# Attention on one core: VectorE's score units placed in ScalarE's sets of PSUM banks, and half of x turned by TensorE

## The chip, the cores and the metric

The kernel runs on one core of a Trainium2 chip. Five engines work side by side, each with its own queue of instructions in a fixed order: TensorE (PE in the profile; its weight loads are PEld), VectorE (DVE), ScalarE (ACT), GpSimd (POOL) and SyncE (SP), which here issues most of the transfers between memory and the core's SBUF. Matmuls write to PSUM, eight banks of 512 fp32 columns on 128 partitions. Semaphores order the engines against each other. The metric is the time of one execution on the device in microseconds (us); lower is better.

## The reference

Two attention blocks over the same x (2048 rows of 512 columns, bf16), each with its own weights, 32 heads of 16 columns, are mixed by a gate of each row.

```python
# block A: full softmax attention, no mask
scores = jnp.einsum("bhqd,bhkd->bhqk", q, k) * (Dh ** -0.5)
p = _softmax(scores, axis=-1)
o = jnp.einsum("bhqk,bhkd->bhqd", p, v)            # then @ A_wo
# block B: each row looks at itself and at 7 rows before it, two apart
W, dil = 8, 2
logits = jnp.einsum("bhsd,bhswd->bhsw", q, kg) * scale   # masked before row 0
attn = _softmax(logits, axis=-1)
o = jnp.einsum("bhsw,bhswd->bhsd", attn, vg)       # then @ B_wo
# the mix
g = _sigmoid((x * gate_w).sum(-1, keepdims=True))
return g * a + (1 - g) * b
```

Block A's exponentials are the bulk: 32 heads x 2048 x 2048.

## The kernel before

**Units, sets and terms.** Block A is worked in 32 periods (line 1263), each with 512 rows of q and four heads. A unit is the score tile of one head for 128 keys and 512 rows of q: one matmul with 32 rows of the array (a strip) into one PSUM bank. A period has 64 units, so there are 2048. A unit is exponentiated in one of two ways. ScalarE reads a set of neighbouring banks, called ring, in one ACTIVATE with exp and writes pT (`emit_fill` line 1419, `act_source` line 1443). There are two sets in turn, rA of three banks and rB of two. VectorE takes units in groups of four, the four heads of one tile of 128 keys (`make_quad`, line 1559; a quad in the code): a conversion of the scores to integers that are the bits of a bf16 near the exponential (dt<-m_ps, one for each unit), then two integer additions over all four units (dt<-dt, the terms; OFFS and WTS at the top of the kernel), so that three terms with weights approximate the exponential. TensorE multiplies pT by v, or the three terms by v and two weighted copies of v (vd_row), and accumulates in the bank acc. Only the last TD = 4 tiles of keys of a period can go to VectorE, since only for these is there a weighted v.

**Banks.** rA three, rB two, acc one, and two single banks m0 and m1 (shown as m_ps). The single banks serve VectorE's score units, and also all projections of q, k and v, block B's projections and sums, and the output projections.

**Block B.** For each of 16 tiles of 128 rows (`b_tile`, line 896): projections on TensorE, k and v stored to memory and loaded again shifted (ksh, vsh), products and sums on GpSimd, softmax, and the weighted sum over the eight rows as matmuls with an identity (`vsum`, line 1075). From tile RELIEF = 6 on, part of the sums is done by VectorE (lred).

**The head.** x is loaded transposed into xT by eight transposing DMAs (`x_load`, line 596). The first weights come on ScalarE's queue into w0 and are rearranged by ScalarE. Ten warm matmuls run meanwhile. `k_proj` with first=True (line 686) projects the first heads' k for four quarters of the rows, VectorE takes the largest absolute value of each (kmax_all), ScalarE copies k to kt_all, VectorE applies a bias from the maximum (kadd), and `q_proj` (line 809) gives q, which VectorE spreads over the strips (shuffles and a bit mask). Then the first set can be filled.

**The order.** The Python program plans the whole order: `Sched` (line 167) keeps for each engine a clock, the pending operations with durations and due times, and slots for every buffer; at each step it commits the operation that can start first, or among near ones that with the earliest due time. `Policy` draws a few settings from a seed, one for each stretch of 8 us of the plan (CHOICES, line 69). `pe_source` (line 1352) offers fills and products, `d_source` and `start_quad` (lines 1618, 1527) open a new group of four for VectorE when the estimated work of both engines allows. `zero_pass` (line 1629) adds matmuls with zeros where TensorE would be too idle. The order is fixed when the program is built; at run time each engine runs its queue and waits on semaphores.

Most instructions go through one wrapper, so the profile shows L509 for nearly all of them, and groups are told apart by tiles: ring, m_ps, acc (PSUM), pT, dt, kt_all, qt, xT (SBUF).

Of the kernel before, what the change touches and what calls it, by code (L numbers as in the profile page):

```python
# [20 lines left out]
DH = 16  # L21
NG = 8
W = 8
# [8 lines left out]
TD = 4  # L32
# [48 lines left out]
RELIEF = 6  # L81
# [47 lines left out]
class Policy:  # L129
    __slots__ = ("full", "press", "quads", "backlog", "heed", "near", "shift", "conv", "ring", "rng", "wobble", "warm", "tight", "late", "whole", "split")  # L130

    def __init__(self, seed):
        self.full, self.press, self.quads, self.backlog, self.heed = 5, -2000.0, 3, 3000.0, True
        self.near, self.shift, self.conv, self.ring, self.wobble, self.warm = 60.0, 0.0, -5000.0, 480.0, 0.0, 0.0
        self.tight, self.late, self.whole, self.split = 600.0, 2000.0, False, False
        self.rng = random.Random(seed)
        if seed:
# [16 lines left out]
            self.warm = pick(0.0, 0.04, 0.08, -0.03)  # L154

# [290 lines left out]
def kernel(  # L446
# [143 lines left out]
    S_.t["DVE"] = 2500.0  # L590
    S_.t["ACT"] = 2500.0
# [4 lines left out]
    def x_load(half):  # L596

        def s():
            lo, hi = half * S // 2, (half + 1) * S // 2
            for c in range(DC):  # L600
                SP.dma_start(out=xT[:, c, lo:hi], in_=x2d[lo:hi, c * 128:(c + 1) * 128], transpose=True)
        return s
# [30 lines left out]
    for kind, lo in (("k", D), ("q", 0)):  # L633
        w0[kind] = const.tile([128, DC, G1], BF16, name=f"w{kind}0")
# [11 lines left out]
    load("x0", x_load(0), 8100.0)  # L646
    load("x1", x_load(1), 13600.0)
    ld["x1a"] = S_.add(Op("SP", lambda: None, dur=1.0, due=-8.0, lat=13000.0, name="ld_x1a"))
    load("bw", dma(bw[:], B_wqkv.rearrange("(c p) n -> p c n", p=128)), 20500.0)
# [4 lines left out]
    load("gw", gw_load, 22000.0)  # L654
    load("wv", dma(wv[:, :, G1:D], a_w3[:, :, 2 * D + G1:3 * D]), 24000.0)
# [22 lines left out]
    S_.t["PE"] = 7800.0  # L678
    xt_ops = {sc: [ld[f"x{sc // 2}"]] for sc in range(NC)}
# [6 lines left out]
    def k_proj(m, sc, due, first=False):  # L686
        lent = first and sc >= 2
        if lent and not early:
            early["hold"] = Hold("rB")
        hold = early["hold"] if lent else Hold("m")  # L690
        st = {}

        def part(c0, c1):
            def s():
                if c0 == 0 and lent:
                    if sc == 2:
                        early["ps"] = ps.tile([128, 2, QW], FP32, tag="rB", bufs=1, name="ring")
                    st["pk"] = early["ps"][:, sc - 2, :]
                elif c0 == 0:
                    st["pk"] = misc_ps(hold, [128, QW])[:]  # L700
# [17 lines left out]
        slow = 2 if first and sc == 0 else 1  # L718
        p1 = Op("PE", part(0, 2), mms=COL4 * (2 * slow), deps=([ld["x1a"]] if lent else xt_ops[sc]) + [ld[("k", m)]], due=due, acq=[] if lent and sc > 2 else [hold], not_before=0.0 if first else due - 5000.0,
                begun=[early["op"]] if lent and sc > 2 else [], name="k1")  # L720
        p2 = Op("PE", part(2, DC), mms=COL4 * (2 * slow), deps=[p1] + (xt_ops[sc] if lent else []), due=due, name="k2")
        for o in (p1, p2):
            S_.add(o)
        if first:
            r = S_.add(Op("DVE", red, dur=700.0, deps=[p2], due=due, name="kred"))
            e = S_.add(Op("ACT", evac, dur=650.0, deps=[p2, r] + k_evs.get(m, [])[-1:], due=due, rel=[] if lent and sc == 2 else [hold], name="kev"))
            if lent and sc == 2:
                early["op"] = p1
            if lent and sc > 2:
                early["next"] = p2  # L730
# [78 lines left out]
    def q_proj(c_, f, due):  # L809
# [15 lines left out]
        def evac():  # L825
            st["qt"] = sb(hq, [128, 2, QW], BF16, "qt")
            V.tensor_copy(out=st["qt"][:, 1, :], in_=st["q"][:])
# [3 lines left out]
        def spread():  # L831
            v = st["qt"][:].bitcast(I32)
            V.stream_shuffle(out=v[:, 0, :], in_=v[:, 1, :], mask=LOWER)
            V.stream_shuffle(out=v[:, 1, :], in_=v[:, 1, :], mask=UPPER)

        def fold():
            for b in range(2):
                v = st["qt"][:, b, :].bitcast(U16)
                V.tensor_scalar(out=v, in0=v, scalar1=rowmask[:, b:b + 1], scalar2=None, op0=ALU.bitwise_and)
        ops = [Op("PE", part(0, 2), mms=COL4 * 2, deps=xt_ops[c_] + [ld[("q", f)]], due=due, acq=[hold, hq], name="q1"),  # L840
               Op("PE", part(2, DC), mms=COL4 * 2, due=due, name="q2"),
               Op("DVE", evac, dur=683.0, allow=300.0, rel=[hold], name="qev"),
               Op("DVE", spread, dur=860.0, allow=2000.0, name="qsh"),
               Op("DVE", fold, dur=486.0, lock=True, allow=2000.0, name="qabs")]
        S_.chain(ops)
        qb_ops[(c_, f)] = ops[1]
        for b in range(2):
            qt_ops[(c_, 2 * f + b)] = (ops[-1], hq)
# [47 lines left out]
    def b_tile(t, due):  # L896
# [190 lines left out]
        f = [Op("PE", vsum(c), mms=[("f", None, 132)] * W, allow=4000.0 if c == 0 else -3000.0, acq=[hb, obt_hold[t]] if c == 0 else [],  # L1087
# [127 lines left out]
    def lent_final(tt, due):  # L1215
# [6 lines left out]
        def step(lo, hi):  # L1222
            def s():
                if not lo:
                    lent["ps", tt] = ps.tile([128, 3 - tt, QW], FP32, tag=tag, bufs=1, name="ring")[:, 0, :]
# [126 lines left out]
    def pe_source(e):  # L1352
# [5 lines left out]
        n = 3 if ring_i[0] == 0 else 2  # L1358
        w = S_.slots[res].when()
        us = act_units(n)  # L1360
        if us and w < INF:
# [3 lines left out]
            if r < INF and S_.slots["pTA" if n == 3 else "pTB"].when() < INF:  # L1365
# [3 lines left out]
                op = Op("PE", None, mms=[("r", u[2], 512) for u in us], name="fillA")  # L1369
                op.fn = lambda us=us, res=res, n=n, op=op: emit_fill(us, res, n, op)  # L1370
# [3 lines left out]
        if pv_wait:  # L1374
# [8 lines left out]
            if whole or full:  # L1383
                a = acc_ready(p)
                if a is not None:
                    vs = [vp_ops[(u[1], 4 * periods[p][1] + u[2])].vis for u in batch]
                    if all(v is not None for v in vs):
# [8 lines left out]
                        used = [sum(w >= INF for w in S_.slots[tag].free) for tag in ("pTA", "pTB")]  # L1396
                        outl.append((op, r, batch[0][3] + (2000.0 if sum(used) < S_.policy.full else S_.policy.press)))
# [21 lines left out]
    def emit_fill(us, res, n, op):  # L1419
# [6 lines left out]
        op.acq = [ring, us, res, n]  # L1426

    def after_fill(op):
        ring, us, res, n = op.acq
# [11 lines left out]
        filled.append(dict(ring=ring, us=us, res=res, n=n, vis=op.vis))  # L1441

    def act_source(e):
# [3 lines left out]
        tag = "pTA" if f_["n"] == 3 else "pTB"  # L1447
# [6 lines left out]
        def fn():  # L1454
            f_["hold"] = Hold(tag)
            f_["hold"].k = S_.slots[tag].take()
            pT = sb(f_["hold"], [128, f_["n"], QW], BF16, "pT")
# [3 lines left out]
        def after(o):  # L1461
            filled.pop(0)
            S_.slots[f_["res"]].give(0, o.vis)
# [55 lines left out]
    quad_at = [0]  # L1519
    quad_end = [None]  # L1520
# [38 lines left out]
    def make_quad(p, t, late):  # L1559
# [6 lines left out]
        aops, fops = [], []  # L1566
        heads = [0, 1, 2, 3]

        def strip():
            after = {u[2] for u in act_units(3 if ring_i[0] == 0 else 2)}  # L1570
            return min(heads, key=lambda j: (max(S_.pe_busy[j], S_.t["PE"]), j in after, j))
        for n_ in range(4):
            hold = Hold("m")
            st = {}

# [4 lines left out]
            def fill(n_=n_, hold=hold, st=st):  # L1580
# [3 lines left out]
                st["s"] = misc_ps(hold, [128, QW])  # L1584
                for _ in range(f_.zeros):
                    mm_pass(st["s"], True, True)
                mm(st["s"][:], kt_all[32 * j:32 * j + 32, i, t * 128:(t + 1) * 128],
                   qt_tiles[periods[p]][32 * j:32 * j + 32, :], True, True, tile_position=(32 * j, 0))

            def conv(n_=n_, st=st):  # L1590
                if n_ == 0:
                    term_tile()
                V.tensor_scalar(out=q["terms"][0][:, st["j"], :], in0=st["s"][:], scalar1=EXP_MULT, scalar2=EXP_ADD,
# [17 lines left out]
        def done(o):  # L1611
            d_busy[0] -= 1
            q["vis"] = o.vis
            pvd_ready.append(q)
# [3 lines left out]
    def d_source(e):  # L1618
        if e == "PE" and d_busy[0] < S_.policy.quads:
# [3 lines left out]
            if dve + max(0.0, S_.t["DVE"] - S_.now) < S_.policy.backlog and S_.now > 22000.0:  # L1623
# [5 lines left out]
    def zero_pass(now):  # L1629
# [5 lines left out]
        if p is None and not front[0]:  # L1635
            mm_pass(ps.tile([128, 3, QW], FP32, tag="rA", bufs=1, name="ring")[:, 0, :], True, True)
# [66 lines left out]
    reds0 = [k_proj(0, sc, 30.0 + sc, first=True) for sc in range(NC)]  # L1703
    k_rows(0, reds0, 40.0, 1, 35000.0)
# [38 lines left out]
```

## Time and profile before

| | |
|---|---|
| time, median of 3 runs | 744.76 us (744.65 to 745.12) |
| the profiled execution | 744.69 us, its span 742.9 us |
| busy: PE, DVE, ACT, POOL | 695.6, 652.9, 719.2, 436.0 us |
| exponentials on ScalarE (pT<-ring) | 626 instructions, 711.7 us |
| conversions on VectorE (dt<-m_ps) | 484 instructions, 319.8 us |
| terms on VectorE (dt<-dt) | 242 instructions, 166.2 us |
| first exponential, end of the last one | 19.46 us, 732.20 us |
| mean granted TensorE clock | 1.000 |

The span runs from the first to the last instruction; the time holds about 1.8 us more. Rows give tiles as out<-in, then the shape, the count, the busy time together, the mean of one in ns, and the idle time of the engine just before them with what ended it. The mean of one holds its latency, during which the next has begun already; where the pace matters, starts are compared with starts.

### The profile page before, as it was taken

What the parts mean: (1) busy time and instruction counts of PE and PEld (TensorE: products, weight loads), DVE (VectorE), ACT (ScalarE), POOL (GpSimd) and SP (SyncE); (2) the same over time, 40 slices, a digit from 0 to 9 for tenths busy, and PEclk for the clock granted to TensorE, in tenths of its full rate; (3) what the DMA queues carried; (4) which work ended last, traced back from release to release, by engine and by line L of the source; (5) the groups of instructions that cost most, each with busy time, mean ns of one, the idle gap of its engine ahead of it and who ended that gap; (6) DMA issues with size and microseconds to landing.
All of it is one profiled execution on the core that took longest, in us unless ns stands there. A gap on an engine that the chain in (4) does not pass through costs nothing.

```text
span 742.9 us, 19546 instructions
## 1 busy us (share of the span) xinstructions
PE 695.6 (94%) x8110; PEld 247.9 (33%) x8110; DVE 652.9 (88%) x1177; ACT 719.2 (97%) x658; POOL 436.0 (59%) x456
## 2 busy tenths in 40 slices
PE   8899999999999989999999999999999999999897
PEld 2332332323323323333323333333333333323233
DVE  3888999798898898989999999989998988897963
ACT  2999999999999999999999999999999999999994
POOL 1066455756556666666655656657656557666660
PEclk9999999999999999999999999999999999999999
DMA  9413020120331201212132311121131113222100
GB/s 217 132 20 119 2 72 2 61 70 15 96 49 59 72 2 60 69 58 73 57 77 25 115 35 39 58 73 58 57 101 58 63 53 102 73 72 71 59 30 29
DMA packets 76232, 47.42 MB, mean 64 GB/s; under 512 B 37232, under 2 KB 73584, under 8 KB 76144
## 3 DMA queue, kind: packets, MB, share of 16 engines
q1 hardware_dynamic: 74288, 45.52, 20.9%
q8 instruction: 63, 1.03, 0.6%
q10 hardware_dynamic: 1856, 0.66, 0.3%
q14 instruction: 25, 0.20, 0.1%
HBM read 37.75 MB, written 6.32 MB: 59 GB/s over the span
## 4 chain that ended last, share of the span: by engine, by line
ACT 64%; PE 17%; issue 15%; DVE 5%; DVEq 0%; ACTq 0%
ACT pT L509 63%; PE m_ps L509 6%; PE acc L509 5%; PE ring L509 5%; DVE dt L509 2%; PE warm L509 1%; ACT lg L509 1%; DVE kt_all L509 0%; DVE accT L509 0%; DVE qt L509 0%; DVE kmax_all L509 0%; DVE lg L509 0%; DVE qb L509 0%; ACT kt_all L509 0%; DVE kvs L509 0%
## 5 line engine op out<-in xcount | busy, mean ns | idle before, releaser
L509 ACT ACTIVATE pT<-ring 128x1536 bf16<-128x1536 f32 x626 | 711.7, 1391 | 0.6 <-PE ring L509 0.4
L509 DVE TENSOR_SCALAR dt<-m_ps 128x512 uint16<-128x512 f32 x484 | 319.8, 680 | 32.8 <-PE m_ps L509 18.8
L509 PE MATMUL ring<-qt,kt_all 32*128 32x512 bf16 x1564 | 255.5, 381 | 36.1 <-ACT pT L509 28.8
L509 POOL TENSOR_TENSOR prod<-ksh,qb 128x512 f32<-128x512 bf16 x128 | 146.0, 1157 | 118.1 <-DVE dt L509 104.3
L509 PEld LDWEIGHTS <-kt_all 32*128 32x128 bf16 (+1 forms) x2304 | 99.9, 91 | 282.4 <-issue 265.1
L509 POOL TENSOR_TENSOR vsh<-vsh,lg 128x512 bf16<-128x512 bf16 x128 | 137.9, 1099 | 64.4 <-DVE dt L509 54.3
L509 DVE TENSOR_SCALAR dt<-dt 128x2048 uint16<-128x2048 uint16 x242 | 166.2, 702 | 3.6 <-PE acc L509 2.0
L509 PE MATMUL m_ps<-qt,kt_all 32*128 32x512 bf16 x484 | 165.3, 382 | 3.3 <-DVE dt L509 1.6
L509 PE MATMUL acc<-pT,vp_row 128*32 128x512 bf16 x1564 | 153.3, 387 | 0.7 <-DVE accT L509 0.3
L509 POOL TENSOR_TENSOR prod<-prod 128x512 f32<-128x512 f32 x88 | 96.2, 1101 | 41.1 <-DVE dt L509 35.6
L509 PEld LDWEIGHTS <-vp_row 128*32 128x32 bf16 x2048 | 49.9, 94 | 100.2 <-issue 91.2
L509 PE MATMUL acc<-dt,vd_row 128*32 128x512 bf16 x968 | 79.8, 381 | 0.0
L509 PE MATMUL m_ps<-bw,xT 128*32 128x512 bf16 x768 | 55.1, 382 | 0.1
L509 PE MATMUL acc<-dt,vp_row 128*32 128x512 bf16 x484 | 48.0, 386 | 1.1 <-DVE accT L509 1.1
L509 PEld LDWEIGHTS <-xT 128*32 128x32 bf16 (+1 forms) x1152 | 32.9, 96 | 27.3 <-issue 19.4
L509 POOL TENSOR_TENSOR ott<-accT,rden 128x256 bf16<-128x256 f32 x31 | 19.7, 635 | 33.8 <-DVE dt L509 28.0
L509 PE MATMUL m_ps<-ident,vsh 128*128 128x128 bf16 x512 | 37.4, 220 | 0.0
L509 PEld LDWEIGHTS <-vsh 128*128 128x128 bf16 x512 | 28.7, 98 | 11.8 <-issue 10.6
L509 PEld LDWEIGHTS <-vd_row 128*32 128x32 bf16 x968 | 25.0, 96 | 21.9 <-issue 9.3
L509 PE MATMUL acc<-ones_t,zw 128*32 128x512 bf16 x332 | 30.7, 387 | 0.0
L509 DVE TENSOR_REDUCE lg<-prod 128x32 f32<-128x512 f32 x40 | 26.5, 672 | 0.0
L509 DVE CAST kvs<-m_ps 128x512 bf16<-128x512 f32 x32 | 21.5, 675 | 4.6 <-PE m_ps L509 4.5
(79 smaller groups left out, 363.1 us busy)
## 6 DMA issues: line engine op xcount, KB each, us to landing
ksh<-kv_scr SPq DMA_DIRECT2D x16, 1024.0 KB, 5.7
vsh<-kv_scr SPq DMA_DIRECT2D x16, 1024.0 KB, 5.4
kv_scr<-kvs SPq DMA_DIRECT2D x16, 256.0 KB, 2.1
out_dram<-osb SPq DMA_DIRECT2D x14, 128.0 KB, 1.7
bw<-in_B_wqkv_dram SPq DMA_DIRECT2D x1, 1536.0 KB, 8.1
bwo<-in_B_wo_dram SPq DMA_DIRECT2D x1, 512.0 KB, 7.2
woarr<-in_A_wo_dram SPq DMA_DIRECT2D x8, 64.0 KB, 2.3
wv<-in_A_wqkv_dram SPq DMA_DIRECT2D x1, 384.0 KB, 8.6
```

Of the source, the lines that this page charges most:

```text
L509: return chain_on(key, f(*a, **k))
```

## The change

VectorE's score units can ride in ScalarE's sets. When TensorE fills a set and a group of VectorE is open whose next unit is ready, `rider` picks it and the set is filled with two units for ScalarE and this one in its third bank; VectorE's conversion reads the bank there (dt<-ring). The set is given back when both have read it (`ring_read`). For this rB has three banks too, and only one single bank, m, is left. The condition is that VectorE's conversion would end within 900 ns (Policy.ride) of the time at which the fill is seen. pT has six buffers of three banks in place of three of three and three of two. TD goes from 4 to 5, RELIEF from 6 to 3, and the seeds of the stretches are others (one fewer).

In the head, the first half of the rows of x is loaded by two plain DMAs into xn and turned by TensorE with the identity into PSUM, then copied to xT by ScalarE and VectorE (`x_turn`); the other half comes by four transposing DMAs, of 1024 rows each. The weights' rearranging moves from ScalarE to GpSimd, w0 lies in buffers that are used later for something else, there are seven warm matmuls accumulating in one bank, the first q is copied by ScalarE and spread in two steps, and the planner's times for loads and for the start of VectorE's groups are earlier. The weighted sums of block B's last two tiles get an earlier due time.

```diff
-TD = 4
+TD = 5
-RELIEF = 6
+RELIEF = 3
+        self.ride = 900.0
...
-    for name_, n_ in (("m", 2), ("rA", 1), ("rB", 1), ("acc", 1), ("pTA", 3), ("pTB", 3), ("qt", 2), 
+    NPT = 6
+    for name_, n_ in (("m", 1), ("rA", 1), ("rB", 1), ("acc", 1), ("pT", NPT), ("qt", 2), 
...
+    PLAIN = 2
+    xn = work.tile([128, PLAIN * TPC, D], BF16, name="xn", tag="ksv_0", bufs=1)
+    def xn_load(q):
+        def s():
+            SP.dma_start(out=xn[:, TPC * q:TPC * (q + 1), :], in_=x2d[q * QW:(q + 1) * QW, :].rearrange("(p t) c -> p t c", t=TPC))
+        return s
+    def x_load(c0, c1):
+        def s():
+            for c in range(c0, c1):
+                SP.dma_start(out=xT[:, c, PLAIN * QW:S], in_=x2d[PLAIN * QW:S, c * 128:(c + 1) * 128], transpose=True)
+        return s
...
-            A.copy(out=o[:, c], in_=_ap(src[:, c, :], [list(src.ap[0]), [DH, 4], [4 * DH, 2], [1, DH]]))
+            G.tensor_copy(out=o[:, c], in_=_ap(src[:, c, :], [list(src.ap[0]), [DH, 4], [4 * DH, 2], [1, DH]]))
...
-    for k in range(10):
-        jt = ps.tile([128, QW], FP32, tag="acc", bufs=1, name="warm")
-        mm(jt[:], ones_t[:, 0:128], ones_t[:], True, True)
+    jt = ps.tile([128, QW], FP32, tag="acc", bufs=1, name="warm")
+    for k in range(7):
+        mm(jt[:], ones_t[:, 0:128], ones_t[:], k == 0, k == 6)
...
+                for k, c in enumerate(cs):
+                    o = st["ps"][:, k, :].rearrange("d (p t) -> d t p", t=TPC)
+                    for tt in range(TPC):
+                        mm(o[:, tt, :], xn[:, TPC * q + tt, c * 128:(c + 1) * 128], ident[:], True, True)
...
+    x_turn(0, (("rA", (0, 1, 2), "ACT"), ("acc", (3,), "DVE")))
+    x_turn(1, (("rB", (0, 1, 2), "DVE"), ("m", (3,), "ACT")))
...
+        d1 = [ld["x2a"]] if first and sc >= PLAIN else xt_ops[sc]
+        p1 = Op("PE", part(0, 2), mms=COL4 * 2, deps=d1 + [ld[("k", m)]], due=due, acq=[hold], not_before=0.0 if first else due - 5000.0, name="k1")
+        p2 = Op("PE", part(2, DC), mms=COL4 * 2, deps=[p1] + xt_ops[sc], due=due, name="k2")
...
-        f = [Op("PE", vsum(c), mms=[("f", None, 132)] * W, allow=4000.0 if c == 0 else -3000.0, acq=[hb, obt_hold[t]] if c == 0 else [],
+        f = [Op("PE", vsum(c), mms=[("f", None, 132)] * W, allow=(4000.0 if t < NT - 2 else 0.0) if c == 0 else -3000.0, acq=[hb, obt_hold[t]] if c == 0 else [],
...
+                with_ = rider(us, max(r, S_.t["PE"])) if n == 3 and len(us) == 3 else None
+                if with_ is not None:
+                    us = us[:2]
...
+    def rider(us, at):
+        if not S_.policy.ride or S_.now < 17500.0:
+            return None
+        for q in quads_open:
+            k = next((k for k in range(4) if q["fops"][k].start is None), None)
+            if k is None:
+                continue
+            f_ = q["fops"][k]
+            if k == 0 and S_.slots["dt"].when() > at:
+                return None
+            if any(d.vis is None or d.vis > at for d in f_.deps) or any(d is not None and d.start is None for d in f_.begun):
+                return None
+            S_.guesses = {}
+            vis = at + 440.0
+            free = max(vis, S_.t["DVE"], S_.guess(q["aops"][k - 1]) if k else 0.0)
+            if free + 683.0 > vis + S_.policy.ride:
+                return None
+            used = {u[2] for u in us[:2]}
+            j = min(q["heads"], key=lambda j: (j in used, S_.pe_busy[j], j))
+            return f_, j, q, k
+        return None
...
+        if with_ is not None:
+            conv = take_ride(op, ring, with_)
+            q, j = with_[2], with_[1]
+            mm(ring[:, 2, :], kt_all[32 * j:32 * j + 32, periods[q["p"]][1], q["t"] * 128:(q["t"] + 1) * 128],
+               qt_tiles[periods[q["p"]]][32 * j:32 * j + 32, :], True, True, tile_position=(32 * j, 0))
...
+    def ring_read(f_, t):
+        f_["reads"] -= 1
+        f_["free"] = max(f_["free"], t)
+        if not f_["reads"]:
+            S_.slots[f_["res"]].give(0, f_["free"])
```

More of the change, by code (lines that the diff above doesn't have):

```diff
@@ L129 @@
 class Policy:
-    __slots__ = ("full", "press", "quads", "backlog", "heed", "near", "shift", "conv", "ring", "rng", "wobble", "warm", "tight", "late", "whole", "split")
+    __slots__ = ("full", "press", "quads", "backlog", "heed", "near", "shift", "conv", "ring", "rng", "wobble", "warm", "tight", "late", "whole", "split", "ride")
     def __init__(self, seed):
@@ L154, in __init__ @@
             self.warm = pick(0.0, 0.04, 0.08, -0.03)
+            self.ride = pick(900.0, 700.0, 1100.0)
     def move(self):
@@ L686, in k_proj @@
     def k_proj(m, sc, due, first=False):
[L687 to L690, printed above, removed]
+        lent = first and sc < PLAIN
+        tag = ("rA", "rB")[sc] if lent else "acc" if first and sc == NC - 1 else "m"
+        hold = Hold(tag)
         st = {}
@@ L694, in s @@
             def s():
[L695 to L700, printed above, removed]
+                if c0 == 0:
+                    st["pk"] = ps.tile([128, 3, QW], FP32, tag=tag, bufs=1, name="ring")[:, 0, :] if lent else ps.tile([128, QW], FP32, tag="acc", bufs=1, name="p1")[:] if tag == "acc" else misc_ps(hold, [128, QW])[:]
                 pk = st["pk"]
@@ L725, in k_proj @@
             r = S_.add(Op("DVE", red, dur=700.0, deps=[p2], due=due, name="kred"))
[L726 to L729, printed above, removed]
+            e = S_.add(Op("ACT", evac, dur=650.0, deps=[p2, r], due=due, rel=[hold], name="kev"))
+            if sc == NC - 1:
                 early["next"] = p2
@@ L826, in evac @@
             st["qt"] = sb(hq, [128, 2, QW], BF16, "qt")
-            V.tensor_copy(out=st["qt"][:, 1, :], in_=st["q"][:])
+            (A.copy if first else V.tensor_copy)(out=st["qt"][:, 1, :], in_=st["q"][:])
             for b in range(2):
                 qt_tiles[(c_, 2 * f + b)] = st["qt"][:, b, :]
[L831 to L834, printed above, removed]
@@ L836, in fold, with spread @@
-        def fold():
-            for b in range(2):
[L838 to L844, printed above, removed]
+        def spread(bs):
+            def s():
+                v = st["qt"][:].bitcast(I32)
+                for b in bs:
+                    V.stream_shuffle(out=v[:, b, :], in_=v[:, 1, :], mask=(LOWER, UPPER)[b])
+            return s
@@ new lines, in fold, with s @@
+        def fold(bs):
+            def s():
+                for b in bs:
+                    v = st["qt"][:, b, :].bitcast(U16)
+                    V.tensor_scalar(out=v, in0=v, scalar1=rowmask[:, b:b + 1], scalar2=None, op0=ALU.bitwise_and)
+            return s
+        ops = [Op("PE", part(0, 2), mms=COL4 * 2, deps=xt_ops[c_] + [ld[("q", f)]], due=due, acq=[hold, hq], name="q1"),
+               Op("PE", part(2, DC), mms=COL4 * 2, due=due, name="q2")]
+        if first:
+            ops.append(Op("ACT", evac, dur=600.0, due=due, rel=[hold], name="qev"))
+            for b in range(2):
+                ops += [Op("DVE", spread([b]), dur=470.0, due=due + 60.0 * b, name="qsh"),
+                        Op("DVE", fold([b]), dur=285.0, lock=True, due=due + 60.0 * b, name="qabs")]
+        else:
+            ops += [Op("DVE", evac, dur=683.0, allow=300.0, rel=[hold], name="qev"),
+                    Op("DVE", spread((0, 1)), dur=860.0, allow=2000.0, name="qsh"),
+                    Op("DVE", fold((0, 1)), dur=486.0, lock=True, allow=2000.0, name="qabs")]
@@ L847, in q_proj @@
         for b in range(2):
-            qt_ops[(c_, 2 * f + b)] = (ops[-1], hq)
+            qt_ops[(c_, 2 * f + b)] = (ops[4 if first and not b else -1], hq)
     g_done = []
@@ L1224, in s @@
                 if not lo:
-                    lent["ps", tt] = ps.tile([128, 3 - tt, QW], FP32, tag=tag, bufs=1, name="ring")[:, 0, :]
+                    lent["ps", tt] = ps.tile([128, 3, QW], FP32, tag=tag, bufs=1, name="ring")[:, 0, :]
                 for q in range(lo, hi):
@@ L1364, in pe_source @@
                 r = max(r, qt_ops[periods[p]][0].vis, kdep(p, t).vis if kdep(p, t).vis is not None else INF)
-            if r < INF and S_.slots["pTA" if n == 3 else "pTB"].when() < INF:
+            if r < INF and sum(w_ < INF for w_ in S_.slots["pT"].free) > len(filled):
                 act_idle = S_.t["ACT"]
@@ L1395, in pe_source @@
                         op.after = lambda o, p=p, batch=batch: after_pva(o, p, batch)
-                        used = [sum(w >= INF for w in S_.slots[tag].free) for tag in ("pTA", "pTB")]
-                        outl.append((op, r, batch[0][3] + (2000.0 if sum(used) < S_.policy.full else S_.policy.press)))
+                        used = sum(w_ >= INF for w_ in S_.slots["pT"].free) + len(filled)
+                        outl.append((op, r, batch[0][3] + (2000.0 if used < NPT - 1 + S_.policy.full - 5 else S_.policy.press)))
         for q in pvd_ready:
@@ L1417, in pe_source, with take_ride, emit_fill @@
         return outl
-    def emit_fill(us, res, n, op):
+    def rider(us, at):
[19 more added lines that the diff above has]
+        return None
+    def take_ride(op, ring, with_):
+        f_, j, q, k = with_
+        q["heads"].remove(j)
+        st = q["sts"][k]
+        st["j"], st["s"] = j, ring[:, 2, :]
+        S_.pend["PE"].remove(f_)
+        for h in f_.acq:
+            if h.res != "m":
+                h.k = S_.slots[h.res].take()
+        f_.start, f_.fin, f_.vis = op.start, op.fin, op.vis
+        conv = q["aops"][k]
+        conv.rel = []
+        return conv
+    def emit_fill(us, res, n, op, with_):
         ring = ps.tile([128, n, QW], FP32, tag=res, bufs=1, name="ring")
@@ L1440, in after_fill @@
         S_.slots[res].take()
-        filled.append(dict(ring=ring, us=us, res=res, n=n, vis=op.vis))
+        f_ = dict(ring=ring, us=us, res=res, n=n, vis=op.vis, reads=1 + (conv is not None), free=0.0)
+        if conv is not None:
+            conv.after = lambda o: ring_read(f_, o.vis)
+        filled.append(f_)
+    def ring_read(f_, t):
[3 more added lines that the diff above has]
+            S_.slots[f_["res"]].give(0, f_["free"])
     def act_source(e):
@@ L1462, in after @@
             filled.pop(0)
[L1463 removed]
+            ring_read(f_, o.vis)
             grp = dict(tag=tag, k=f_["hold"].k, n=nu, pT=f_["pT"])
@@ L1622, in d_source @@
             dve = sum(o.dur for o in S_.pend["DVE"] if S_.est(o) is not None)
-            if dve + max(0.0, S_.t["DVE"] - S_.now) < S_.policy.backlog and S_.now > 22000.0:
+            if dve + max(0.0, S_.t["DVE"] - S_.now) < S_.policy.backlog and S_.now > 17500.0:
                 start_quad()
@@ L1635, in zero_pass @@
         if p is None and not front[0]:
+            if S_.slots["rA"].when() > now:
+                return False
             mm_pass(ps.tile([128, 3, QW], FP32, tag="rA", bufs=1, name="ring")[:, 0, :], True, True)
@@ L1700, in after_post @@
                 final(c_, tt, NPR - 1, NPR, now)
-    reds0 = [k_proj(0, sc, 30.0 + sc, first=True) for sc in range(NC)]
-    k_rows(0, reds0, 40.0, 1, 35000.0)
-    q_proj(0, 0, 35.0)
+    reds0 = [k_proj(0, sc, 40.0 + sc, first=True) for sc in range(NC)]
+    k_rows(0, reds0, 50.0, 1, 35000.0)
+    q_proj(0, 0, 40.5)
     for tb in (0, 8):
```

84 lines of the change are left out of this document (53 added, 31 removed), and 16 rows, old and new, of the table CHOICES.

## The prediction

> **What bounds the kernel now.** I read the page first (engines, chain, groups), then the groups by form for ScalarE, the waits, and the timeline of the two ends.
>
> ```profile
> span 742.9 us, 19546 instructions
> PE 695.6 (94%) x8110; PEld 247.9 (33%) x8110; DVE 652.9 (88%) x1177; ACT 719.2 (97%) x658; POOL 436.0 (59%) x456
> ACT 64%; PE 17%; issue 15%; DVE 5%; DVEq 0%; ACTq 0%
> L509 ACT ACTIVATE pT<-ring 128x1536 bf16<-128x1536 f32 x626 | 711.7, 1391 | 0.6 <-PE ring L509 0.4
> L509 DVE TENSOR_SCALAR dt<-m_ps 128x512 uint16<-128x512 f32 x484 | 319.8, 680 | 32.8 <-PE m_ps L509 18.8
> ```
>
> ScalarE is busy 97% of the span and its exponentials alone take 711.7 us with 0.6 us of idle time before them. Whatever shortens the kernel must shorten that row, or let it begin or end earlier. By form:
>
> ```profile
> L509 ACT ACTIVATE pT<-ring 128x1536 bf16<-128x1536 f32 x313 | 502.8, 1606 | 0.5 <-PE ring L509 0.4
> L509 ACT ACTIVATE pT<-ring 128x1024 bf16<-128x1024 f32 x312 | 367.3, 1177 | 0.1
> ```
>
> 313 sets of three units, 312 of two, one of one: 1564 units, and 484 go to VectorE. Single rows overlap their successors, so I take start-to-start: in the trace a three-unit set starts its successor a median of 1331 ns later, a two-unit set 904 ns. So a unit costs 427 ns and a set 50 ns. 1564 x 0.427 + 626 x 0.050 = 699.1 us; 16 small exponentials of the local block (307 ns each) add 4.9; the rest of the 712.7 us between 19.46 and 732.20, some 8.5 us, is sets that started later than their median. The waits:
>
> ```profile
> PE ring L509 <- ACT pT L509: 28.8, 90, 0.8
> DVE dt L509 <- PE m_ps L509: 18.8, 36, 1.4
> DVE dt L509 <- PE ring L509: 11.7, 20, 1.7
> PE m_ps L509 <- DVE dt L509: 1.6, 6, 0.4
> ```
>
> TensorE waits for ScalarE to free a set. VectorE waits for TensorE, hardly ever the other way round (1.6 us). The two ends, in the timeline:
>
> ```profile
> 0.72 11.14 SPq L509 DMA_TRANSPOSE xT<-in_A_x_dram  x8
> 9.49 1.09 PE L509 MATMUL m_ps<-xT,wkd 128*32 128x512 bf16 x8
> 13.06 1.04 PE L509 MATMUL p<-xT,wqd 128*32 128x512 bf16 x16
> 14.60 1.91 PE L509 MATMUL ring<-xT,wkd 128*32 128x512 bf16 x32
> 19.46 5.97 ACT L509 ACTIVATE pT<-ring 128x1536 bf16<-128x1536 f32 x5 [0.44 <-PE ring L509]
> 731.34 1.96 PE L509 MATMUL m_ps<-ident,vsh 128*128 128x128 bf16 x32
> 733.23 0.40 PE L509 MATMUL acc<-pT,vp_row 128*32 128x512 bf16 x4
> 739.80 0.39 ACTq L509 DMA_DIRECT2D out_dram<-kt_all  x1
> ```
>
> So: 19.5 us of head before ScalarE starts, 712.7 us in which it sets the pace, 10.7 us of tail. For the head also the DMA issues and two windows of 2 us (last: DMA share of the 16 engines, GB/s):
>
> ```profile
> xT<-in_A_x_dram SPq DMA_TRANSPOSE x8, 4.0
> 4.00:6.00 2.00, 1.81 (x4) 0.37 (x4) 0.00 (x0) 1.39 (x7) 0.00 (x0) 1.00 1.28 254
> 16.00:18.00 2.00, 1.55 (x44) 1.00 (x36) 1.71 (x5) 0.05 (x1) 0.00 (x0) 1.00 0.97 365
> ```
>
> The transposing loads keep the engines full at a lower rate than the plain load of bw behind them.
>
> **The head.** Eight transposing loads take SP 11.14 us to issue (1.39 each) and land 4.0 us after their issue begins; the last lands at 14.2 and the first exponential starts 5.3 us later. Four are replaced by two plain loads (issue 0.58 each by the bw row), so issue alone would put the last landing near 0.7 + 1.2 + 3 x 1.39 + 4.0 = 10.1. But from 2 to 14 us the DMA share reads 0.95 to 1.28 in every 2 us, so the engines may be the limit: 0.39 MB of weights at 240 GB/s (1.6), 1.05 MB plain at 340 as the bw load gets (3.1), 1.05 MB transposed at 189 (262 KB in 1.39 us: 5.6), after 2 us: 12.3. I take 11.1. Behind the landing stood 32 projections (1.91); half of those now wait only for the first two transposes, so 0.9 goes: first exponential at 11.1 + 5.3 - 0.9 = 15.5. Three chains must fit before it. VectorE: casts of one and three banks (0.68, 1.75), four maxima (2.76), the two spreads and folds of q (1.5), the bias and its application (1.1): 7.8 us from about 7. TensorE: seven warm matmuls in one bank, 32 turning matmuls (61 ns at the rate of the vsh row: 2.0), projections. Eight k matmuls at 9.49 took as long as sixteen of q at 13.06, though the granted clock reads 1.00 throughout: TensorE runs at half pace until about 12. If that stays so, turning and early projections cost 1.8 + 2.6 more. POOL's eight weight copies, 0.4 each by its 128x128 mask row, end near 7 and are hidden by the load of x. **Head: -4.0** (ends -1.5 with half pace and saturated DMA, -5.0 with issue alone).
>
> By the Trainium skill, "TensorE: Matmul & The Clock Gate", Part 1, about 3.4 us of sustained matmuls lift the half rate. The trace shows half pace after 8 us of gappy warm matmuls (0.60 each with a pause); the gapless ones of the change would then be through it by about 5 us, and the head would be -4.5 as an estimate. The Trainium skill, "DMA: Bandwidth & Descriptors", Latency and other measured facts, gives 261 GB/s for transposing loads; the trace has 189, and by the page the head would be an estimated 1.6 us better.
>
> **The sets.** Both are now three banks. A set with a rider gives ScalarE two units and VectorE the third. With R riders and N units on ScalarE there are (N + R)/3 sets. VectorE uses one conversion per 1.5 us, ScalarE starts a set every 1.14 us, so most could ride, but the single bank takes some and a rider must be ready just then: I take R = 300. With N = 1552 (below) that makes 617 sets, 9 fewer: **-0.5** (R = 0: 517, -5.4; all 496 riding: 683, +2.8).
>
> **VectorE's share.** Up to five tiles a head group instead of four may now go to VectorE; 121 groups of four units (242 second-and-third-term instructions, two a group) of 128 were used, so the cap was near. A group costs VectorE 4 + 2 instructions at 0.60 start-to-start, 3.6 us, and saves ScalarE 1.71. VectorE was idle 90 us. Of that, three more tiles whose sums move from POOL (RELIEF 6 to 3) take 12 x 0.59 = 7.1; the fifth weighted tile 0.6; a span shorter by 8 takes 8. The conversions' own wait of 32.8 us should fall by half where they ride, since their fill comes with ScalarE's; waits of the other evacuations (some 30 us: projections, local block, output) grow when one single bank serves them, as the next projection can't fill while the last is read. 16 us gained less some 5 lost, divided by 3.6: **three groups more, 12 units, -5.1** (ends: six fewer, +10, where the single bank chokes; nine more, -15.4, where half the idle time is used).
>
> **New waits.** A set is refilled only when both readers are through; behind the waiting fill all of TensorE's queue stands, and ScalarE behind it. The planner rides only where the conversion ends within 900 ns of the fill (Policy.ride), and the two-unit exponential, 904 ns, starts no earlier than that fill, so ScalarE is the last reader unless VectorE is late by the lead of the fill. That lead is some 0.4 us. TensorE's wait for VectorE's m bank was 1.6 us over 484 fills. I add **+2.0** to the 8.5 us of late sets (ends 0 and +14, below). The changed seeds only reorder work; POOL is busy 59% and loses work.
>
> **The tail.** The 32 sums of the last local tile (1.96 us from 731.34) stand ahead of the last accumulation, which starts 1.0 us after the last exponential. They get an earlier due time: **-0.9** (0 to -1.0).
>
> **Sum.** -4.0 - 0.5 - 5.1 + 2.0 - 0.9 = -8.5. The profiled execution took 744.69 us, 1.8 outside its span, 0.07 under the median of 744.76: 736.2 us.
>
> **Rivals.** (1) Slower: coupling. The place is the refill behind a rider. VectorE's conversions started 46 us later in sum than back-to-back, 95 ns each. If half of that reached ScalarE at 300 riders, the new waits would be +14 in place of +2 and the sum +3.5: 748.2. The point from which it decides is a loss of (8.5 + 2)/300 = 35 ns for each rider. Against it: the two-unit cover and the 1.6 us row. Chance 0.20. (2) VectorE fills up: nine groups more, -15.4, less 4.0 and 0.9, +3 for VectorE's late second and third terms: 727.4. For it: 90 us of idle time, and ridden fills save TensorE the switches between row and column tiles. Chance 0.17. (3) The single bank eats what the riders give: no more groups, all ride: -4.0 - 0.9 + 1.0 + 2.0: 742.8. Chance 0.20. (4) The change doesn't do what it says: riders hardly find their conditions. Then 517 sets, -5.4, no more groups: -4.0 - 5.4 + 2.0 - 0.9, 736.4, much the same time for another reason. Chance 0.03. My forecast: 0.40, with its own range 732 to 740.
>
> **How the numbers follow.** A measurement here tells about 0.2% (1.5 us) from no change. Case 1 is slower but for a little; the forecast, (2) and (4) are faster; of (3), 0.16 is faster, 0.02 within and 0.02 slower. Faster 0.76, same 0.02, slower 0.22. The range leaves out the far half of (2) and the far half of (1): 728 to 748.
>
> **What would show it.** First pT row at 15.5 (14.5 to 18). Forms of pT: about 300 of 1024 columns and 317 of 1536. dt from ring about 300, from m_ps some 200, 248 term rows. TensorE's ring wait for DVE dt, which had none, under 5 us. VectorE's busy share over 90%. Last exponential near 724.5. The prediction is wrong if sets start late on average by more than 35 ns a rider, if VectorE keeps its 90 us of idle time, or if the first exponential stays past 18.

## The result and the profile after

The changed kernel takes 954.9 us (median of 4 runs, 952.66 to 957.28) against 744.94 us for the kernel before in the same comparison: a ratio of 1.282 (95% interval 1.279 to 1.285), 210 us slower. The forecast was 736.2 us, with 728 to 748 as its range. The profiled execution took 954.59 us, with a span of 952.8.

The page of the changed kernel: engines, granted clock, chain, and the groups that answer to those shown of before.

```profile
span 952.8 us, 19593 instructions
PE 779.6 (82%) x8163; PEld 265.2 (28%) x8163; DVE 682.6 (72%) x1220; ACT 744.2 (78%) x675; POOL 422.2 (44%) x449
PEclk8779879788998597879877979987896877989999
ACT 33%; DVE 31%; PE 25%; issue 10%; ACTq 0%; DVEq 0%
L511 ACT ACTIVATE pT<-ring 128x1024 bf16<-128x1024 f32 (+1 forms) x648 | 732.6, 1191 | 190.5 <-DVE dt L511 141.6
L511 DVE TENSOR_SCALAR dt<-ring 128x512 uint16<-128x512 f32 x396 | 267.1, 686 | 225.6 <-ACT pT L511 196.8
L511 DVE TENSOR_SCALAR dt<-m_ps 128x512 uint16<-128x512 f32 x104 | 70.5, 678 | 4.3 <-PE ring L511 2.5
```

No engine is full any more: ScalarE 78%, VectorE 72%, TensorE 82%. Before, ScalarE had 64% of the chain that ended last and VectorE 5%; now they have 33% and 31%, so the end is set by the two in turn. The work is near the forecast: 396 units rode (300 forecast), 104 went through the single bank (some 200), and 648 sets were exponentiated (617). What is new is the idle time before both groups. Its causes, in the waits (engine and tile that waited, engine and tile waited for, us, times, longest):

```profile
DVE dt L511 <- ACT pT L511: 196.8, 171, 2.2
ACT pT L511 <- DVE dt L511: 141.6, 137, 1.7
PE ring L511 <- ACT pT L511: 87.5, 141, 1.3
PE ring L511 <- DVE dt L511: 61.1, 124, 1.4
ACT pT L511 <- PE ring L511: 42.8, 84, 1.4
```

The first two rows did not exist before. VectorE's conversion waits for ScalarE's exponential, and ScalarE's exponential for VectorE's conversion, although neither reads what the other writes. How it runs, in the timeline of the changed kernel:

```profile
302.00 0.39 PE L511 MATMUL ring<-qt,kt_all 32*128 32x512 bf16 x3
...
302.44 0.69 DVE L511 TENSOR_SCALAR dt<-ring 128x512 uint16<-128x512 f32 x1
...
303.01 0.39 PE L511 MATMUL ring<-qt,kt_all 32*128 32x512 bf16 x3
...
303.22 2.85 ACT L511 ACTIVATE pT<-ring 128x1024 bf16<-128x1024 f32 x3 [0.26 <-DVE dt L511]
...
305.19 0.69 DVE L511 TENSOR_SCALAR dt<-ring 128x512 uint16<-128x512 f32 x1 [1.47 <-ACT pT L511]
...
305.94 0.39 PE L511 MATMUL ring<-qt,kt_all 32*128 32x512 bf16 x3 [1.25 <-DVE dt L511]
...
306.43 1.45 ACT L511 ACTIVATE pT<-ring 128x1536 bf16<-128x1536 f32 x1 [0.35 <-PE ring L511]
```

The set filled at 302.00 is read by the conversion at 302.44, and its exponential starts only behind it, at 303.22. In the next set, filled at 303.01, it is the other way round: VectorE is idle for 1.47 us until that set's exponential is through, and converts at 305.19. The fill at 305.94 waits 1.25 us for that conversion, and the next exponential for the fill. The two readings of one set, meant to run side by side, run one behind the other. (A row with x3 holds three exponentials, each of another set.)

The waits are in the program itself. Its list of VectorE's instructions shows them, with the engine whose semaphore each waits for:

```
200 L511 TensorScalarPtr dt<-ring 128x512 [waits Activation_49]
201 L511 TensorScalarPtr dt<-dt 128x2048 [waits DVE_49]
202 L511 TensorScalarPtr dt<-ring 128x512 [waits Activation_49]
203 L511 TensorScalarPtr dt<-dt 128x2048
204 L511 TensorCopy kvs<-m_ps 128x512 [waits PE_49]
205 L511 TensorScalarPtr dt<-ring 128x512 [waits PE_49] x2
```

The kernel's own plan asks for no such wait. The framework that turns tiles into semaphores has put the two readings of a set in order, though both only read and their banks differ. A set is one tile of three banks, which is presumably why. Of the 396 pairs the reader that comes second in the program waits for the first: 222 times it is the conversion, 174 times the exponential.

### The profile page after: what moved, and what is told of

Read it like the earlier page. It is cut to its first block, busy times and chain, and to the rows that moved or that the text cites. A ratio compares the mean times of both kernels' runs of the same rounds, so it can differ in the third digit from the quotient of the medians.

```text
span 952.8 us, 19593 instructions
## 1 busy us (share of the span) xinstructions
PE 779.6 (82%) x8163; PEld 265.2 (28%) x8163; DVE 682.6 (72%) x1220; ACT 744.2 (78%) x675; POOL 422.2 (44%) x449
## 4 chain that ended last, share of the span: by engine, by line
ACT 33%; DVE 31%; PE 25%; issue 10%; ACTq 0%; DVEq 0%
ACT pT L511 33%; DVE dt L511 24%; PE ring L511 10%; PE acc L511 8%; PE m_ps L511 7%; DVE qt L511 1%; DVE kt_all L511 1%; DVE lg L511 1%; DVE accT L511 1%; DVE kvs L511 1%; DVE qb L511 0%; DVE kmax_all L511 0%; PE warm L511 0%; ACTq L511 0%; DVE oat L511 0%
## 5 line engine op out<-in xcount | busy, mean ns | idle before, releaser
L511 ACT ACTIVATE pT<-ring 128x1024 bf16<-128x1024 f32 (+1 forms) x648 | 732.6, 1191 | 190.5 <-DVE dt L511 141.6
L511 DVE TENSOR_SCALAR dt<-ring 128x512 uint16<-128x512 f32 x396 | 267.1, 686 | 225.6 <-ACT pT L511 196.8
L511 PE MATMUL ring<-qt,kt_all 32*128 32x512 bf16 x1944 | 302.3, 435 | 153.1 <-ACT pT L511 87.5
L511 PE MATMUL acc<-pT,vp_row 128*32 128x512 bf16 x1548 | 173.1, 439 | 4.3 <-ACT pT L511 3.0
L511 POOL TENSOR_TENSOR prod<-prod 128x512 f32<-128x512 f32 x76 | 83.2, 1098 | 83.0 <-DVE dt L511 77.0
L511 PE MATMUL acc<-dt,vd_row 128*32 128x512 bf16 x1000 | 91.5, 432 | 0.0
L511 DVE TENSOR_SCALAR dt<-m_ps 128x512 uint16<-128x512 f32 x104 | 70.5, 678 | 4.3 <-PE ring L511 2.5
L511 PE MATMUL m_ps<-bw,xT 128*32 128x512 bf16 x768 | 63.8, 435 | 1.9 <-DVE kvs L511 1.0
L511 PE MATMUL m_ps<-qt,kt_all 32*128 32x512 bf16 x104 | 46.2, 445 | 4.6 <-DVE dt L511 1.5
L511 PE MATMUL acc<-ones_t,zw 128*32 128x512 bf16 x340 | 39.3, 488 | 0.0
```

What stands on the lines that cost most here:

```text
L511: return chain_on(key, f(*a, **k))
```

## The experiments

**The order between the two readers taken away.** The framework lets a kernel declare that a given dependency need not be kept. Here each pair is declared, and nothing else is touched: the instructions of every engine and their order are those of the changed kernel, and the refill still waits for both readers. No data can go wrong by it, since both only read, and different banks.

```diff
+    def reader(f_, what, bi):
+        f_[what] = bi
+        if "exp" in f_ and "conv" in f_:
+            other = f_["exp" if what == "conv" else "conv"]
+            tc.declare_no_dep(bi.ins, other.ins, reason="two readers of different banks")
...
-            A.activation(out=pT[:, 0:nu, :], in_=f_["ring"][:, 0:nu, :], func=ACT.Exp, scale=float(DH) ** -0.5)
+            bi = A.activation(out=pT[:, 0:nu, :], in_=f_["ring"][:, 0:nu, :], func=ACT.Exp, scale=float(DH) ** -0.5)
+            reader(f_, "exp", bi)
...
+                if "set" in st:
+                    reader(st["set"], "conv", bi)
```

> The changed kernel with one thing else: the order between a set's two readers (ScalarE's exponential and the rider's conversion, which read different banks) is declared void, so neither waits for the other; every engine's instructions and their order stay the same, and the refill still waits for both. Theory A (the two readers of one set are put in order by semaphore waits, and that alone costs the 210 us): 730 to 748 us, granted clock 0.99 or more, no wait of pT for dt over 5 us in sum and none of dt for pT. Theory B (the readers slow each other on the chip, or the lower granted clock of TensorE is the cause and the waits follow from it): above 900 us, clock near 0.86.

Measured: 736.88 us (736.23 to 737.49) against 744.87 before, a ratio of 0.989 (0.987 to 0.991), granted clock 0.991. It is 218 us faster than the changed kernel with the same instructions, and about 1.1% faster than the kernel before, a small gain but one clear of the interval. The page, and two rows of ScalarE by form:

```profile
span 735.5 us, 19595 instructions
PE 674.6 (92%) x8163; PEld 249.9 (34%) x8163; DVE 670.5 (91%) x1220; ACT 715.1 (97%) x675; POOL 423.3 (58%) x449
ACT 75%; issue 13%; PE 11%; DVE 2%; ACTq 0%; DVEq 0%
L511 DVE TENSOR_SCALAR dt<-ring 128x512 uint16<-128x512 f32 x396 | 266.6, 680 | 19.4 <-PE ring L511 15.6
```

```profile
L511 ACT ACTIVATE pT<-ring 128x1024 bf16<-128x1024 f32 x396 | 405.3, 1169 | 1.2 <-PE ring L511 0.7 <-PE m_ps L511 0.4
L511 ACT ACTIVATE pT<-ring 128x1536 bf16<-128x1536 f32 x252 | 379.5, 1592 | 2.0 <-PE ring L511 2.0
```

ScalarE is full again and has 75% of the chain; the wait of each reader for the other is gone from the waits. So theory A holds. Nor do the two readers slow each other: a set of two units starts its successor a median of 904 ns later and one of three 1330 ns (904 and 1331 before), a conversion a median of 601 ns (601 before). The Trainium skill, "PSUM — Partial Sum Buffer", Specifications (TRN2), says that ScalarE and VectorE can access PSUM in parallel at full rate as long as they don't meet in a bank; these rows agree with it.

**No riders at all.**

```diff
-        self.ride = 900.0
+        self.ride = 0.0
...
-            self.ride = pick(900.0, 700.0, 1100.0)
+            self.ride = 0.0 * pick(900.0, 700.0, 1100.0)
```

> The changed kernel with riding switched off in the planner: sets are always three units of ScalarE, VectorE's score units all go through the one single bank. Theory A: no set has two readers, so the loss is gone: 740 to 775 us (the single bank gives VectorE fewer units than 500, ScalarE more), clock 0.99 or more. Theory B: with one reader for each set also faster than 900, but if the lower clock comes from the new head or from the single bank, still 850 or more with a clock near 0.86.

Measured: 889.73 us (median of three runs, 887.17 to 898.97; a fourth took 901.03), ratio 1.197 (1.190 to 1.205), granted clock 0.953 in the profiled one of 898.97. Theory A missed. Of theory B the time came true (850 to 900, if the single bank or the new head is to blame), but not the clock near 0.86. The two rows of its groups that tell why, and its waits:

```profile
L511 ACT ACTIVATE pT<-ring 128x1536 bf16<-128x1536 f32 x571 | 773.7, 1610 | 85.4 <-PE ring L511 84.6
L511 DVE TENSOR_SCALAR dt<-m_ps 128x512 uint16<-128x512 f32 x336 | 229.9, 684 | 138.2 <-PE m_ps L511 97.2
```

```profile
DVE kvs L511 <- PE m_ps L511: 44.0, 27, 2.7
DVE kt_all L511 <- PE m_ps L511: 29.4, 17, 3.5
DVE osb L511 <- PE m_ps L511: 22.7, 14, 3.0
```

There is no pair here, and it is still 145 us slower than before, for reasons other than the order of readers. VectorE waits 97 us for its units in the single bank and tens of us for each kind of projection, gets only 84 groups (336 units) in place of 121, and ScalarE has to take 1712 units. These 148 units more, in 55 sets fewer, cost ScalarE some 60 us (148 x 0.427 - 55 x 0.050); another 85 us are waits for a set to be filled, 27 of them, up to 10.6 us long. What kept TensorE from these fills was not followed up. The head, the limits of the plan and its seeds differ from the kernel before too, and the seeds were not chosen for a plan without riders; how much a better choice would mend was not tried. So it does not give a price of the single bank alone. What it shows is that in this plan the riders are no extra on top of two three-bank sets: the single bank is bearable only with them.

**One direction at a time.** In the same place, only pairs of one order are freed.

```diff
-        if "exp" in f_ and "conv" in f_:
+        if what == "exp" and "conv" in f_:
```

> Of the pairs in a set only those where the exponential stands second in the program (174 of 396) are freed: the exponential no longer waits for the conversion; in the other 222 the conversion still waits for the exponential. Theory A: the 142 us that pT waits for dt goes, the wait of dt for pT stays or grows: 800 to 900 us. Theory B: above 930 us.

Measured: 801.08 us, clock 0.984. The other way round:

```diff
-        if "exp" in f_ and "conv" in f_:
+        if what == "conv" and "exp" in f_:
```

> The other half: the 222 conversions that stand second no longer wait for the exponential; 174 exponentials still wait for the conversion. Theory A: the 197 us of dt waiting for pT goes, and the exponentials then wait less too, because the conversions come earlier: 760 to 850 us. Theory B: above 930 us.

Measured: 799.01 us, clock 0.973. Both are theory A's by the range; of free_conv I had expected the more to go because it takes the larger wait away, and the two came out alike. So 222 conversions waiting cost 64 us (801.1 - 736.9), 174 exponentials waiting 62 us, and both together 218 us, far more than the sum. What makes up the rest was the next question.

**Is it the clock?** The granted clock is 0.857 in the changed kernel and 0.991 in the freed one. To lift it without moving any other instruction, four matmuls by zero follow nearly every fill that carries a rider (360 of 396).

```diff
+            p0 = last_acc[0]
+            if p0 is not None and npv[p0] > 0:
+                mm_pass(acc_tiles[periods[p0]], False, False)
         op.acq = [ring, us, res, n, conv]
```

> The changed kernel, its waits between a set's readers as they are, with four matmuls by zero into acc put behind every fill that carries a rider (360 passes, 0.215 us each at full rate), unknown to the planner, so that every other instruction keeps its place. TensorE then works where it would wait. Theory C (the lower granted clock, 0.86, follows from TensorE's waits and makes a large part of the loss, which is why the two halves of the waits cost 64 and 62 us alone but 218 together): clock 0.96 or more and 830 to 890 us. Theory D (the waits alone make the loss, the clock only goes with it): the clock rises too, but the time stays at 930 or more.

> The same zero passes in the kernel whose readers don't wait for each other (736.9 us without them), as a control for what the passes cost in themselves: TensorE has some 60 us idle there and the passes take 77, so both theories expect 738 to 790 us, clock 0.99 or more.

Measured: 930.5 us at a clock of 0.972 with the waits, and 761.3 us at 1.000 in the freed kernel. In the freed kernel the passes cost 24 us (761.3 - 736.9); with the waits the kernel gained 24 us (954.9 - 930.5). If the passes cost the same in both, the higher clock is worth up to some 49 us of the 218; the rest stays at a nearly full clock, and the waits with it:

```profile
span 928.7 us, 22473 instructions
ACT 36%; DVE 34%; PE 16%; issue 12%; SPq 1%; DMA 1%; ACTq 0%; DVEq 0%
```

```profile
DVE dt L511 <- ACT pT L511: 183.2, 167, 2.7
ACT pT L511 <- DVE dt L511: 136.3, 134, 1.7
```

Theory C, that the clock makes the large part, falls; it is nearer to theory D. What a lower clock costs where no set has two readers was asked of the kernel before, without its zero matmuls:

```diff
-    S_.filler = zero_pass
+    S_.filler = None
```

> The kernel before without the planner's zero matmuls (its 86 passes and what the plan puts in their place): the price of a lower clock where no set has two readers. Theory C: clock below 0.98 and 750 to 800 us. Theory D: the clock may fall, the time stays within 740 to 750 us.

Measured: 801.42 us at a clock of 0.897, 57 us slower than before though no set has two readers. This run does not isolate the clock, since the planner also made another order: VectorE takes 472 units in place of 484, which by the prices of before costs ScalarE some 5 us, and ScalarE now waits 39.9 us for sets to be filled (0.4 before), while TensorE's matmuls into the sets take a mean of 417 ns (381 before). That the slower TensorE makes most of the loss fits these rows, but is argued. In the changed kernel there is presumably less for it to take, since the engines stand waiting for each other anyway; that was not measured.

**Is it the mixture of directions?** Every second pair of either order is freed, in one kernel the even ones, in the other the odd ones.

```diff
+            seen[what] += 1
+            if seen[what] % 2 == 0:
+                return
             other = f_["exp" if what == "conv" else "conv"]
```

> Every second pair of either order freed, so that 111 conversions still wait for the exponential and 87 exponentials for the conversion: 198 waits in both directions, between the 222 of free_exp and the 174 of free_conv that go in one direction only and cost 64 and 62 us. Theory E (one direction is partly absorbed, since the engine that never waits runs ahead; waits in both directions make the two engines take turns, and that is why 396 cost 218): 830 to 880 us. Theory F (the cost grows with the number of waits more than in proportion, whatever their direction): 790 to 810 us.

> The same with the other half of the pairs kept (111 and 87 again). Theory E: 830 to 880 us. Theory F: 790 to 810 us. The two halves within 20 us of each other by both.

Measured: 859.5 us (clock 0.938) and 873.0 us (0.921). So 198 waits in both directions cost 123 and 136 us, twice what 222 or 174 cost in one. Both runs lie in theory E's range and outside theory F's. Their clock is lower too (0.938 and 0.921, against 0.984 and 0.973 with one direction), but by the price above, up to 49 us from 0.857 to 0.972, in proportion an estimated 27 us at most, and not the 60 to 75 us between them. The waits of the first of the two:

```profile
DVE dt L511 <- ACT pT L511: 109.5, 103, 2.3
ACT pT L511 <- DVE dt L511: 68.2, 81, 1.6
```

With only the exponentials freed, the same view has 81.4 us for 222 conversions that wait:

```profile
DVE dt L511 <- ACT pT L511: 81.4, 161, 1.6
PE ring L511 <- DVE dt L511: 71.1, 154, 1.3
ACT pT L511 <- PE ring L511: 39.6, 117, 1.1
```

Fewer waits, and yet more waiting, as soon as the other engine waits too. The last two rows show how one direction alone reaches ScalarE: the late conversion holds up the refill, and the refill the next exponential. My reading, which no run shows by itself: in one direction one engine runs on and the other is late only behind it, so part of the wait falls into time that it had to spare; in both directions each engine's lateness is handed to the other and comes back with the next set.

## Why the prediction was wrong

The step that failed is "New waits", the term of +2.0. It asked only when a set can be refilled, and priced VectorE's lateness there (+2.0, with +14 as its end). It took for granted that the two readers of a set run side by side, since they read different banks and the planner starts them independently. In the program the second waits for the first (196.8 us of conversions waiting, 141.6 us of exponentials waiting), and that costs 218 us. The first rival, coupling at the refill, had the right sign but not this place: its price was worked out from conversions that start late, and a wait of one reader for the other was not in it. Nothing in the trace of before shows two engines reading one set in the attention stage, so the bounds should have asked what a second reader of a tile is made to wait for.

The freed kernel has the same instructions, and against it each other term can be read off:

- **Head:** forecast first exponential at 15.5, a gain of 4.0. In the freed kernel it starts at 15.93, a gain of 3.5; in the changed kernel at 16.54. The number came near, but not by the path that was added up, so this is in part luck. The forecast let the landing of the last transposing load (11.1 us) set the time. The chain that leads to the first exponential of the freed kernel holds no transposing load; it holds the warm and the turning matmuls to 8.85 us, the projections, and VectorE's maxima and spreads. Four of its steps, and the instructions:

```profile
4.60 2.06 PE ring L511 x12
9.82 0.89 PE p L511 x16
13.00 1.18 DVE kmax_all L511 x2
15.02 0.42 DVE kt_all L511
```

```profile
1.65 7.89 SPq L511 DMA_TRANSPOSE xT<-in_A_x_dram  x4
...
4.46 2.20 PE L511 MATMUL ring<-ident,xn 128*128 128x128 bf16 x12
...
6.89 1.51 PE L511 MATMUL ring<-ident,xn 128*128 128x128 bf16 x12
...
9.65 1.04 PE L511 MATMUL p<-xT,wqd 128*32 128x512 bf16 x16
...
15.93 1.45 ACT L511 ACTIVATE pT<-ring 128x1536 bf16<-128x1536 f32 x1 [1.12 <-PE ring L511]
```

The 32 turning matmuls took 4.4 us (4.46 to 8.85 us) in place of 2.0. From start to start the first ones took 213 ns each, and from about 5.9 us on all took 109 ns, where the vsh row had promised 61. The step from 213 to 109 is that from half pace to full pace: the k and q projections behind them ran at full pace. It came at about 7.1 us in the changed kernel, and in half_a, whose head has the same instructions, all 32 already ran at 109 ns, from 4.91 us on:

```profile
4.91 1.48 PE L511 MATMUL ring<-ident,xn 128*128 128x128 bf16 x12 [0.50 <-DMA xn<-in_A_x_dram]
```

So the early full rate that I drew from "TensorE: Matmul & The Clock Gate", Part 1, of the Trainium skill was there by 5 us in half_a, and about 1 and 2 us later in the freed and the changed kernel. The larger part of the error is the price of a turning matmul at full pace. Why it is 109 ns and not 61 is not shown; both kinds load weights for each matmul, but a turning matmul writes every fourth column of its bank, and a vsh sum neighbouring columns. The 1.6 us that the transposing rate of "DMA: Bandwidth & Descriptors", Latency and other measured facts, of the Trainium skill promised did not show either. The four transposing loads took 7.9 us to issue, 1.97 each, and none stands in the chain.

- **Sets:** 396 rode, not 300, so 648 sets in place of 617: +1.1 against -0.5. Within the ends.
- **VectorE's share:** 125 groups (250 term rows, two each), four more than before where three were forecast: 16 units, -6.8 against -5.1.
- **Late sets, without the order of readers:** the sets' starts lie 10.9 us above their medians in the freed kernel (9 ns on average after 241 sets of three, 22 ns after 389 of two) against 8.5: +2.4 against +2.0. The refill is no problem, as the forecast had it (under 5 us of TensorE waiting for a rider's conversion); the waits of the freed kernel have:

```profile
PE ring L511 <- DVE dt L511: 0.4, 2, 0.2
```

- **Tail:** from the end of the last exponential at 725.50 to the span's end at 735.5, 10.0 us against 10.7: -0.7 against -0.9. The 32 sums still stand ahead of the last accumulation; they only begin earlier.

Together -3.5 + 1.1 - 6.8 + 2.4 - 0.7 = -7.5, and 744.7 - 7.5 = 737.2; the freed kernel's profiled execution took 737.3. Two rivals were priced wrongly. The third, that the single bank eats what the riders give, has +1.0 for sets in which all ride, where the forecast's own price for that is +2.8; its sum would be 744.6. The fourth, hardly any riders, was put at 736.4, much the same time as the forecast; without riders the kernel took 889.73, and VectorE lost 37 groups, where the forecast's worst end was six.

## What to carry to other kernels

Before two engines share one tile, look in the built program at what each instruction waits for: the framework may order two reads of one PSUM tile even where they touch different banks, and a plan of one's own that doesn't know of it can lose more than it gains (here 218 us). Count such waits by direction: here some 200 waits between two engines cost twice as much when they ran in both directions as when they ran in one. Where a forecast for a change of structure rests on two things running at once, the trace must show the two at once somewhere, or the bounds must hold the case that they don't.

## What the runs showed that was not expected

The changed kernel without riders, in which one single bank serves everything, is 145 us slower than the kernel before (889.7 against 744.9 us). The kernel before without its zero matmuls is 57 us slower (801.4 against 744.9 us, clock 0.897 against 1.000), though its plan is another one too. And the same instructions at the head of one kernel do not take the same time in every run: TensorE's step from half to full pace came anywhere from before 4.9 us (half_a) to about 7.1 us (the changed kernel), and the first exponential at 15.79 and 16.54 us.
